# Group 0's outputs in the Strassen scheme of the other groups, x sums inside it, mixes on the vector engine, last keys ahead of the scan

## The chip, the core and the metric

The kernel runs on one core of a Trainium2 chip. The core has five engines, each with an instruction queue of its own that it works off in order: PE (matrix products; the profile lists weight loads apart as PEld), DVE (vector), ACT (scalar), POOL (GpSimd) and SP, which here only issues transfers. They wait for each other through semaphores. SBUF is the on-chip memory with 128 partitions, PSUM the banks that PE writes to. The metric is the device time of one execution in microseconds, as a median over runs.

## What is computed

An attention block with a gated recurrence, and then a feed-forward block with three input weights:

```
f = sigmoid(f_logit)                       # batch 4, heads 8, time 768, head size 48
state = f[t][:, None] * state + outer(k[t], v[t])
y[t]  = q[t] @ state
x   = y as (3072 tokens, 384)
h   = max(x @ w1, x @ w2, x @ w3)          # w1, w2, w3: 384 x 768
out = h @ w_out                            # w_out: 768 x 384
```

The weights arrive as 64-bit floats; each is turned into 32 bits on the chip ("rounding").

## The kernel before

**Units.** The recurrence is worked off in 24 units `u` of 64 time steps by two batches (128 tokens). For a unit, `scan` turns the gates on DVE and forms their running products, `after` makes `kh` (keys times decay) and `before` makes `qh` (queries times decay); from unit 6 on both products are on POOL (L340, L351), and the keys, queries and gates are turned by DVE transposes (L296). `pairs` multiplies `kh` and `qh` on PE (L392) and masks the result on DVE into `at` (L395). `values` multiplies `at` by v (L411), `sums` brings the state up to date from the turned keys `ks` (L436), `finish` adds the old state's part (L500) and copies the result to `xT`. `ks` is made by `keys_by_blocks(u, n)` for n = 0 to 3, four DVE transposes of 32 rows each (L382).

**Groups.** Four units are a group of 512 tokens. The feed-forward block of a group is a Python generator that yields the cost of each piece of PE work; `fill(ns)` in the unit loop (L1023 to L1075) pulls pieces until its budget is used up, so PE's order is units' products with feed-forward pieces between. A unit has five fills: of EARLY = 2360 while group 0 is worked off (units 4 to 7), of PART after. All is in one hand-written order; nothing is moved by a scheduler.

**The first matrix is subtracted.** The maximum is taken relative to x @ w1: w2 and w3 are replaced by w2 - w1 and w3 - w1 (`apart`), h is the maximum of their products and 0, and x @ w1 @ w_out is added by one linear matrix w1 @ w_out, which `linear` computes on PE from turned pieces of w1 (`turn`). It is kept as `w_nat`, and as `w_lin` with its rows placed in the order of heads by `place`, a set of ten small copies that SP issues. `place` also puts w2 and w3 (`w_in[1]`, `w_in[2]`) into `placed[0]` and `placed[1]`, while `linear` runs.

**Group 0** (`ffn_first`): plain products for w2 and w3, rounding of the last weight pieces (`round_to`), `turn`, `linear`, then `outputs`: per 128 tokens nine products with 384 columns, six with w_out and three with `w_nat`, a copy on ACT and a store. Between these outputs POOL makes `mix_in` (four sums of placed input weights, L805) and `mix` (five differences of output weights, L587), for use from group 1 on.

**Groups 1 to 5** (`ffn`): `inputs_by_pairs` (L836) and `outputs_by_pairs` (L609) use Strassen's scheme, seven products of half-size matrices in place of eight, over the halves of h's rows and the halves of w_out's columns. Its mixed weights are `w_mix`, kept in the space of `w_in[2]` and one tile of their own; its mixed h are `s_mix`, in the space of `w_in[1]`, made by `sums_of_hm` with four POOL operations per pair of h blocks (L596). The linear part, x by `w_lin`, is added by plain products, three per tile: 66 products of 192 columns per group. Sums that a product needs twice are copied from PSUM by ACT (`read`, L614) into `partial`, and added by DVE (`add`, L617) or POOL (L662). The products accumulate in the PSUM banks a, b, c; a is written on after it is read.

**What sets the order around the change.** SP issues all transfers in program order. DVE's order in a unit is: `ks` parts 0, 1 and 2, `at`, gate, scan, `ks` part 3, turned keys, second scan, turned queries, state.

Of the kernel before, what the change touches and what calls it, by code (L numbers as in the profile page):

```python
# [9 lines left out]
FP32 = mybir.dt.float32  # L10
# [3 lines left out]
ALU = mybir.AluOpType  # L14
# [32 lines left out]
C = 64  # L47
# [8 lines left out]
def kernel(  # L56
# [12 lines left out]
    nc = tc.nc  # L69
# [8 lines left out]
    GRP = 4  # L78
# [11 lines left out]
    def fast():  # L90
        ctx = ExitStack()
        with ctx:
# [137 lines left out]
            BY_VECTOR = 3  # L230
# [3 lines left out]
            def round_begin(n):  # L234
                if n in raw:
                    lo, hi = words(n)
                    top = tops[:, n % 4].bitcast(U32)
                    if n >= BY_VECTOR:

                        nc.scalar.activation(top.bitcast(FP32), hi.bitcast(FP32), AF.Sign)  # L240
                        nc.scalar.mul(top.bitcast(FP32), top.bitcast(FP32), -2.0)

                    rest = rests[:, n % 3].bitcast(U32)
                    nc.scalar.activation(rest, lo, AF.Copy, scale=2.0 ** -29)
                    halfway[n] = (top, rest)

            def round_end(n):
                if n in raw:
                    (top, rest), (_, hi) = halfway.pop(n), words(n)
                    if n < BY_VECTOR:  # L250
                        nc.vector.tensor_scalar(top, hi, 3, 0x3FFFFFF8, op0=ALU.logical_shift_left, op1=ALU.bitwise_and)
                        nc.vector.scalar_tensor_tensor(top, hi, 0xC0000000, top, op0=ALU.bitwise_and, op1=ALU.bitwise_or)
                    else:
                        nc.vector.scalar_tensor_tensor(top, hi, 3, top, op0=ALU.logical_shift_left, op1=ALU.bitwise_xor)  # L254

                    dst = pieces[n][0].bitcast(U32)
                    by = lambda t: t.rearrange("p (a c) -> p a c", a=dst.shape[1])
                    nc.gpsimd.tensor_tensor(dst, by(top), by(rest), op=ALU.add)  # L258
                    raw.pop(n)
# [297 lines left out]
            def outputs(hm, xT, i):  # L557
                p = bank()
                t = slice(i % 2 * UT, (i % 2 + 1) * UT)
                terms = [(hm[:, j, i * UT:(i + 1) * UT], w_out[:, j, :]) for j in range(NJ)]  # L560
                terms += [(by_halves(xT)[:, i // 2, k, t], w_nat[:, k, :]) for k in range(NK)]
                for n, (lhsT, rhs) in enumerate(terms):
                    nc.tensor.matmul(p[:, 0:DM], lhsT=lhsT, rhs=rhs, start=(n == 0), stop=(n == NJ + NK - 1))  # L563
                    if n % NK == NK - 1:
                        if n == NJ + NK - 1:
                            o = o_four[:, i]
                            nc.scalar.copy(o, p[:, 0:DM])
                            store(i, o)
                        yield NK * DM * COLUMN

            HJ, HD = NJ // 2, DM // 2
            corner = lambda k, n: w_out[:, k::2, n * HD:(n + 1) * HD]
            w_mix = [keep.tile([128, HJ, HD], FP32, name="mix")] + [w_in[2][:, :, n * HD:(n + 1) * HD] for n in range(4)]
            s_mix = [w_in[1][:, n, :].rearrange("q (jj t) -> q jj t", jj=HJ) for n in range(NK)]
            partial = [w_in[0][:, n, 0:DM] for n in range(NK)]
            pairs_of = lambda t: t.rearrange("q (p c) -> q p c", p=2)  # L580

            def mix(n):

                dst, x, y = ((w_mix[2], corner(1, 1), corner(0, 1)), (w_mix[0], corner(0, 1), corner(0, 0)),
                             (w_mix[1], corner(1, 1), w_mix[0]), (w_mix[3], corner(1, 0), w_mix[1]),
                             (w_mix[4], w_lin[:, :, 0:HD], w_lin[:, :, HD:]))[n]
                nc.gpsimd.tensor_tensor(dst, x, y, op=ALU.subtract)  # L587

            def sums_of_hm(hm, jj):

                first, second = ([hm[:, 2 * jj + k].rearrange("q (p n t) -> q n p t", p=2, n=2)[:, n] for n in range(2)]
                                 for k in range(2))
                s1, s2, s4 = (pairs_of(t[:, jj]) for t in s_mix)
                for dst, x, y, op in ((s1, first[1], second[1], ALU.add), (s2, s1, first[0], ALU.subtract),
                                      (first[1], first[0], first[1], ALU.subtract), (s4, second[0], s2, ALU.subtract)):
                    nc.gpsimd.tensor_tensor(dst, x, y, op=op)  # L596

            def outputs_by_pairs(g, hm, xT):
                tile_of = lambda p, n: slice((2 * p + n) * UT, (2 * p + n + 1) * UT)
                A = lambda k, n: lambda p: hm[:, k::2, tile_of(p, n)]  # L600
                X = lambda n: lambda p: xT[:, 0:NK, tile_of(p, n)]
                s1, s2, s4 = (lambda p, t=t: t[:, :, p * UT:(p + 1) * UT] for t in s_mix)
                lin = [w_lin[:, :, n * HD:(n + 1) * HD] for n in range(2)]
# [3 lines left out]
                def into(b, p, lhs, rhs):  # L607
                    for k in range(HJ):
                        nc.tensor.matmul(b[:, p * HD:(p + 1) * HD], lhsT=lhs(p)[:, k], rhs=rhs[:, k],  # L609
                                         start=id(b) not in begun, stop=(k == HJ - 1), skip_group_check=True)  # L610
                        begun.add(id(b))
# [7 lines left out]
                COST = HJ * HD * COLUMN  # L619
                a, b, c = bank(), bank(True), bank(True)  # L620
                into(b, 0, X(0), lin[0])
                yield COST
                into(b, 1, X(0), lin[0])
                yield COST
                into(a, 0, A(0, 0), corner(0, 0))
                yield COST
                into(b, 0, A(1, 0), corner(1, 0))
                yield COST
                into(a, 1, A(0, 0), corner(0, 0))
                read(a, 0)  # L630
                yield COST
                into(b, 1, A(1, 0), corner(1, 0))
# [3 lines left out]
                yield COST  # L636
                into(a, 0, s2, w_mix[1])
                yield COST
                into(a, 1, s2, w_mix[1])
                read(a, 1)  # L640
                yield COST
                d = b if last else c
                into(c, 0, s1, w_mix[0])
# [4 lines left out]
                into(d, 1, s1, w_mix[0])  # L648
# [5 lines left out]
                into(a, 0, A(0, 1), w_mix[2])  # L654
                yield COST
                into(a, 1, A(0, 1), w_mix[2])
                yield COST
                into(a, 0, X(1), lin[1])
                yield COST
# [3 lines left out]
                if last:  # L663
                    store_part(g, 1, 1)
                yield COST
                into(c, 0, X(0), lin[1])
                yield COST
                into(d, 1, X(0), lin[1])
                yield COST
                into(a, 0, A(1, 1), w_mix[3])  # L670
                yield COST
                into(a, 1, A(1, 1), w_mix[3])
# [3 lines left out]
                into(a, 0, X(1), w_mix[4])  # L676
                yield COST
                into(a, 1, X(1), w_mix[4])
# [3 lines left out]
                yield COST  # L682
                into(c, 0, s4, corner(1, 1))
# [3 lines left out]
                into(d, 1, s4, corner(1, 1))  # L687
# [67 lines left out]
            def ffn_first(xT):  # L755
# [18 lines left out]
                for a in range(NK):  # L774
                    if a < 2:
                        for n in range(2 * NK + 2):
                            place(placed[a].bitcast(FP32), w_in[a + 1], n)
                    for cost in linear(a):
                        round_to(rounded[0] + 1)
                        yield cost  # L780
                for n in range(2 * NK + 2):
                    place(w_lin, w_nat, n)
                made = iter([lambda n=n: mix_in(n) for n in range(4)] + [lambda n=n: mix(n) for n in range(5)])
                for i in range(GRP):
                    for n, cost in enumerate(outputs(hm, xT, i)):
                        if i or n:
                            next(made, lambda: None)()
                        if i == GRP - 1 and n == 1 and 1 in packed:
                            sums_of_x(1)
                        yield cost  # L790
# [33 lines left out]
            def inputs_by_pairs(g, hm, xT):  # L824
# [57 lines left out]
                def fourth(n):  # L882
                    into(A[n], n, w_two[1][:, 1], t4)
                    yield COST
                    into(A[n], n, w_two[1][:, 2], t5)
                    nc.vector.scalar_tensor_tensor(out(n, 0), out(n, 0), 0.0, two(A[n]), op0=ALU.max, op1=ALU.max)
                    nc.vector.scalar_tensor_tensor(out(n, 1), out(n, 1), 0.0, u3, op0=ALU.max, op1=ALU.max)  # L887
                    sums_of_hm(hm, n)
                    yield COST
# [48 lines left out]
            EARLY = 2360  # L938
            PART = (33 * TOK + 22 * HJ * HD) * COLUMN / (5 * GRP)
# [4 lines left out]
            with tc.manual_schedule():  # L944
# [78 lines left out]
                for u in range(GRP, NU):  # L1023
# [22 lines left out]
                    if u + 2 < NU:  # L1046
                        load_v(u + 2)
                    if n < NU:
                        if n < BY_ROWS:
                            sigmoids(n)  # L1050
                        scan(n)
                    check_range(u - CHECKS, 0)
                    fill(part)
                    keys_by_blocks(u, 3)
# [293 lines left out]
```

## Time and profile before

| | us |
|---|---|
| median of three runs | 422.57 (422.08 to 423.26) |
| the profiled execution | 423.19 |
| its span, first to last instruction | 421.5 |
| PE busy | 401.8 |
| DVE busy | 275.0 |
| POOL busy | 241.9 |
| ACT busy | 178.8 |
| mean granted clock of PE | 0.994 of full speed |

Stages, from the windows of the profile: up to 86 us the first units and group 0's input products run, with PE busy 71.3 us; from 86 to 98.7 `linear`; to 127 group 0's outputs; then five groups of some 60 us each, of which the outputs take about 25; the last matmul ends at 416.5.

A line of the chain of waits names a start, a length, the engine and source line, and how many instructions were put together. A 32-bit matmul is two records in it. A line of a timeline has the start, the length, the engine, line and operation, output and inputs with their shapes, and in brackets the idle time of the engine ahead of it with what ended that.

### The profile page before, as it was taken

To read this page: it belongs to the slowest core of one execution; us is meant where nothing else is said; L and a number is where in the kernel's file an instruction comes from. 1 tells how busy PE (TensorE), PEld (TensorE's weight loads), DVE (VectorE), ACT (ScalarE), POOL (GpSimd) and SP (SyncE) were. 2 spreads that over 40 slices of the span, in tenths; PEclk is the share of its full clock that TensorE was granted. 3 is DMA by queue.
4 is the path that set the end of the run, shared out by engine and by line. 5 is a ranking of instruction groups with operands and counts; after the bars stand their busy time and mean duration, and the time that the engine had idled before them with its cause. 6 is when DMAs were issued, how large, how long until landed. Compare 5 with 4: busy or idle time off the path is not lost.

```text
span 421.5 us, 11552 instructions
## 1 busy us (share of the span) xinstructions
PE 401.8 (95%) x4618; PEld 336.0 (80%) x4618; DVE 275.0 (65%) x549; ACT 178.8 (42%) x412; POOL 241.9 (57%) x266
## 2 busy tenths in 40 slices
PE   5978898899999999999999999999999999999995
PEld 4766764366668888998889988889988889988994
DVE  6995585897697699868789867889764730002300
ACT  2478576532114442425531444442254524577210
POOL 2189454744998676376586358576556960435600
PEclk9999999899999999999999999999999999999999
DMA  8999886677456763277645276725373010552012
GB/s 169 233 268 268 241 225 92 84 152 153 82 114 90 120 144 54 71 92 110 118 111 110 42 116 80 155 65 94 55 147 94 13 54 10 154 143 75 1 21 60
DMA packets 181562, 47.21 MB, mean 112 GB/s; under 512 B 160448, under 2 KB 179200, under 8 KB 181504
## 3 DMA queue, kind: packets, MB, share of 16 engines
q1 hardware_dynamic: 178032, 45.62, 52.9%
q10 hardware_dynamic: 3472, 0.81, 0.9%
q8 instruction: 37, 0.61, 0.6%
q14 instruction: 21, 0.17, 0.1%
HBM read 37.75 MB, written 4.72 MB: 101 GB/s over the span
## 4 chain that ended last, share of the span: by engine, by line
PE 87%; SPq 3%; DMA 3%; DVE 3%; ACT 1%; issue 1%; POOL 1%; DVEq 0%; ACTq 0%; POOLq 0%
PE p L836 19%; PE tr L836 16%; PE p L609 15%; PE tr L609 12%; PE p L537 6%; PE p L563 6%; PE y L411 3%; PE p L745 3%; PE y L500 3%; PE a L392 2%; PE y L436 2%; SPq L174 2%; DMA raw<-in_moe_w_dram 2%; DMA placed<-in_moe_w_dram 1%; SPq L164 1%
## 5 line engine op out<-in xcount | busy, mean ns | idle before, releaser
L382 DVE STREAM_TRANSPOSE ks<-kh 32x128 f32<-32x128 f32 x256 | 77.4, 302 | 5.1 <-POOL kh L340 1.0
L836 PE MATMUL tr<-xT,placed 128*128 128x256 f32 x300 | 73.4, 385 | 0.0
L836 PEld LDWEIGHTS tr<-xT,placed 128*128 128x128 f32 x300 | 55.6, 190 | 9.1 <-ACT hm L844 1.4
L836 PE MATMUL p<-xT,placed 128*128 128x256 f32 x180 | 45.0, 381 | 0.0
L537 PE MATMUL p<-xT,w_in 128*128 128x256 f32 (+1 forms) x108 | 36.2, 477 | 6.2 <-DVE hm L767 3.5
L340 POOL TENSOR_TENSOR kh<-kt,r 128x512 f32<-128x512 f32 x18 | 31.2, 1732 | 11.4 <-DVE kt L296 11.4
L617 DVE TENSOR_TENSOR o<-tr,w_in 128x384 f32<-128x384 f32 (+1 forms) x11 | 5.7, 514 | 48.8 <-PE tr L609 43.5
L836 PEld LDWEIGHTS p<-xT,placed 128*128 128x128 f32 x180 | 33.8, 190 | 4.7
L329 DVE TENSOR_TENSOR_SCAN r<-gate,from_one 128x520 f32<-128x520 f32 x24 | 31.5, 1312 | 8.2 <-ACT gate L308 5.1
L596 POOL TENSOR_TENSOR w_in<-hm 128x256 f32<-128x256 f32 x15 | 10.9, 724 | 40.2 <-DVE hm L887 40.2
L854 POOL TENSOR_TENSOR hm<-hm,rest_bits 128x512 f32<-128x512 f32 x15 | 23.0, 1533 | 18.8 <-ACT hm L844 18.8
L506 ACT COPY xT<-y 64x256 f32<-64x256 f32 (+1 forms) x60 | 22.1, 368 | 27.2 <-PE y L500 26.6
L537 PEld LDWEIGHTS p<-xT,w_in 128*128 128x128 f32 x108 | 19.9, 195 | 15.4 <-issue 8.6
L347 DVE TENSOR_TENSOR_SCAN prod<-gate,from_inv 128x520 f32<-128x520 f32 x24 | 32.2, 1340 | 0.0
L836 PE MATMUL p<-w_in,placed 128*128 128x256 f32 x120 | 30.0, 379 | 0.0
L258 POOL TENSOR_TENSOR w_in<-top_bits,rest_bits 128x384 uint32<-128x384 uint32 x18 | 22.1, 1233 | 13.1 <-DVE top_bits L254 8.1
L879 DVE TENSOR_TENSOR hm<-tr,hm 128x512 f32<-128x512 f32 x15 | 10.2, 681 | 29.0 <-PE tr L836 19.0
L662 POOL TENSOR_TENSOR o<-top_bits,w_in 128x384 f32<-128x384 f32 x5 | 5.1, 1014 | 41.6 <-ACT w_in L614 41.6
L395 DVE TENSOR_TENSOR at<-a,mask 128x512 f32<-128x512 f32 x24 | 16.5, 688 | 17.8 <-PE a L392 17.4
L614 ACT COPY w_in<-p 128x384 f32<-128x384 f32 x15 | 7.2, 478 | 47.3 <-PE p L609 47.3
L280 ACT ACTIVATE raw<-top_bits 128x384 f32<-128x384 f32 x48 | 25.2, 526 | 0.4
L836 PEld LDWEIGHTS p<-w_in,placed 128*128 128x128 f32 x120 | 22.8, 190 | 3.1
(155 smaller groups left out, 884.5 us busy)
## 6 DMA issues: line engine op xcount, KB each, us to landing
raw<-in_moe_w_dram SPq DMA_DIRECT2D x24, 384.0 KB, 3.9
v_ld<-in_v_dram SPq DMA_DIRECT2D x48, 96.0 KB, 3.2
placed<-in_moe_w_dram SPq DMA_DIRECT2D x12, 384.0 KB, 6.5
out_dram<-o SPq DMA_DIRECT2D x46, 96.0 KB, 2.2
placed<-in_moe_w_out_dram SPq DMA_DIRECT2D x6, 384.0 KB, 5.7
f_ld<-in_f_logit_dram SPq DMA_DIRECT2D x36, 64.0 KB, 2.6
k_ld<-in_k_dram SPq DMA_DIRECT2D x36, 64.0 KB, 2.6
q_ld<-in_q_dram SPq DMA_DIRECT2D x36, 64.0 KB, 2.5
```

The source lines that it names most:

```text
L258: nc.gpsimd.tensor_tensor(dst, by(top), by(rest), op=ALU.add)
L280: nc.scalar.activation(over, size, AF.Relu, scale=(-1 / HI_MIN, 1.0)[step - 1], bias=(1.0, -HI_END * (1 - 2.0 ** -24))[step - 1], accum_ou ...
L329: nc.vector.tensor_tensor_scan(r[:, 0:LEN][:, ::-1], flat(gate)[:, ::-1], flat(from_one)[:, ::-1], 1.0, op0=ALU.mult, op1=ALU.max)
L340: (nc.vector if u < BY_ROWS else nc.gpsimd).tensor_tensor(kh.rearrange("p h a t -> p a h t"), kt, by_batch(r[:, 1:LEN + 1].rearrange("p (x ...
L347: nc.vector.tensor_tensor_scan(flat(prod), flat(gate_tiles[u % 2]), flat(from_inv[u % 2]), 1.0, op0=ALU.mult, op1=ALU.max)
L382: nc.vector.transpose(ks[n * 32:(n + 1) * 32, :, par, e0:e0 + 32], kh[p0:p0 + 32, :, a, t0:t0 + 32])
L506: nc.scalar.copy(xT[o, :, t0 + a * C:t0 + (a + 1) * C], y[i, a, 0:HP * C].rearrange("p (h t) -> p h t", h=HP))
L537: nc.tensor.matmul(p if w < TOK else p.rearrange("p (two t) -> p two t", two=2), lhsT=w_in[i][:, kt, j * 128:(j + 1) * 128], rhs=x[:, t.st ...
L563: nc.tensor.matmul(p[:, 0:DM], lhsT=lhsT, rhs=rhs, start=(n == 0), stop=(n == NJ + NK - 1))
L609: nc.tensor.matmul(b[:, p * HD:(p + 1) * HD], lhsT=lhs(p)[:, k], rhs=rhs[:, k], start=id(b) not in begun, stop=(k == HJ - 1), skip_group_c ...
L836: nc.tensor.matmul(b[:, j * HALF:(j + 1) * HALF], lhsT=w[:, (2 * n + j) * 128:(2 * n + j + 1) * 128], rhs=x, start=begin and j == 0, stop= ...
L854: nc.gpsimd.tensor_tensor(out(n, 0), out(n, 0), first, op=ALU.add)
```

## The change

Group 0's outputs use `outputs_by_pairs` as well, with `mixed` false: h in the scheme and the linear part plain, by `w_nat`. Its `sums_of_hm` on POOL are put between the steps of `linear`, and the five `mix` operations go to DVE, in one block after `linear`; `w_mix[0]` now lies in w_out itself. In groups 1 to 5 two of the three x blocks enter the scheme as a fourth block, with weights `x_mix` (five DVE operations, `mix_x`, once in group 1) and sums of x (`sums_of_x_pair`, four DVE operations per group); only the third block stays plain, which makes 64 products. Inside the scheme the products of the last h block come later, and the s1 products ahead of the s2 products. The six w_out pieces are rounded with two DVE operations in place of two ACT and one DVE, two pieces per step of `linear`. `ks` part 3 goes ahead of the scan. EARLY and PART are made smaller.

```
-            BY_VECTOR = 3
+            BY_VECTOR = (*range(3), *range(3 * NJ, 4 * NJ))
...
-            w_mix = [keep.tile([128, HJ, HD], FP32, name="mix")] + [w_in[2][:, :, n * HD:(n + 1) * HD] for n in range(4)]
+            w_mix = [corner(0, 1)] + [w_in[2][:, :, n * HD:(n + 1) * HD] for n in range(4)]
+            x_mix = [w_lin[:, 0, HD:]] + [w_mix[4][:, n] for n in range(2)] + [keep.tile([128, HD], FP32, name="mix")]
...
+            s_last = keep.tile([128, HALF], FP32, name="s_last")
             def mix(n):
                 dst, x, y = ((w_mix[2], corner(1, 1), corner(0, 1)), (w_mix[0], corner(0, 1), corner(0, 0)),
                              (w_mix[1], corner(1, 1), w_mix[0]), (w_mix[3], corner(1, 0), w_mix[1]),
-                             (w_mix[4], w_lin[:, :, 0:HD], w_lin[:, :, HD:]))[n]
-                nc.gpsimd.tensor_tensor(dst, x, y, op=ALU.subtract)
+                             (w_mix[4], w_nat[:, :, 0:HD], w_nat[:, :, HD:]))[n]
+                nc.vector.tensor_tensor(dst, x, y, op=ALU.subtract)
+            def mix_x(n):
...
+                nc.vector.tensor_tensor(dst, x, y, op=ALU.subtract)
...
+            def sums_of_x_pair(xT, n):
+                sums_of_pair(xT[:, 0], xT[:, 1], *s_of_x(xT), part=slice(2 * n, 2 * n + 2), engine=nc.vector)
...
             def outputs_by_pairs(g, hm, xT):
...
+                mixed = g > 0
+                order = [*range(HJ - 1), *[HJ] * mixed, HJ - 1]
...
+                if mixed:
+                    sums_of_x_pair(xT, 0)
                 into(b, 0, X(0), lin[0])
...
+                early, rest = slice(len(order) - 1), slice(len(order) - 1, None)
+                for p in range(2):
+                    into(a, p, A(0, 0), C(0, 0), early)
+                    if mixed and p:
+                        sums_of_x_pair(xT, 1)
+                    yield COST - PART_COST
+                    into(b, p, A(1, 0), C(1, 0), early)
+                    yield COST - PART_COST
...
-                into(a, 0, s2, w_mix[1])
-                yield COST
-                into(a, 1, s2, w_mix[1])
-                read(a, 1)
-                yield COST
                 d = b if last else c
-                into(c, 0, s1, w_mix[0])
+                into(c, 0, s1, T(0))
...
+                into(a, 0, s2, T(1))
                 yield COST
-                into(a, 1, A(0, 1), w_mix[2])
+                into(a, 1, s2, T(1))
+                read(a, 1)
+                yield COST
+                into(a, 0, A(0, 1), T(2))
+                yield COST
+                into(a, 1, A(0, 1), T(2))
...
             def ffn_first(xT):
...
-                    for cost in linear(a):
-                        round_to(rounded[0] + 1)
+                    for n, cost in enumerate(linear(a)):
+                        round_to(rounded[0] + 2)
+                        if a and n < 2:
+                            jj = 2 * (a - 1) + n
+                            if jj < HJ:
+                                sums_of_hm(hm, jj)
                         yield cost
                 for n in range(2 * NK + 2):
                     place(w_lin, w_nat, n)
-                made = iter([lambda n=n: mix_in(n) for n in range(4)] + [lambda n=n: mix(n) for n in range(5)])
-                for i in range(GRP):
-                    for n, cost in enumerate(outputs(hm, xT, i)):
-                        if i or n:
-                            next(made, lambda: None)()
-                        if i == GRP - 1 and n == 1 and 1 in packed:
-                            sums_of_x(1)
-                        yield cost
+                for n in range(5):
+                    mix(n)
+                for n, cost in enumerate(outputs_by_pairs(0, hm, xT)):
+                    if 3 <= n < 7:
+                        mix_in(n - 3)
+                    yield cost
...
-            EARLY = 2360
-            PART = (33 * TOK + 22 * HJ * HD) * COLUMN / (5 * GRP)
+            EARLY = 2270
+            PART = (33 * TOK + 64 * HD) * COLUMN / (5 * GRP)
...
+                    keys_by_blocks(u, 3)
                     if n < NU:
...
                     fill(part)
-                    keys_by_blocks(u, 3)
```

## The prediction

> **What bounds the kernel now.** I read the page's busy shares first, then a table of windows by stage, then the chain of waits in order of time, then the timelines of the queues in the stage where the change adds waits.
>
> ```profile
> PE 401.8 (95%) x4618; PEld 336.0 (80%) x4618; DVE 275.0 (65%) x549; ACT 178.8 (42%) x412; POOL 241.9 (57%) x266
> ```
>
> ```profile
> 60.00:86.00 26.00, 22.51 (x242) 11.62 (x241) 19.52 (x33) 17.18 (x36) 15.79 (x15) 0.93 0.68 87
> 86.00:98.70 12.70, 12.70 (x161) 7.78 (x160) 12.25 (x29) 2.21 (x6) 6.22 (x6) 1.00 0.77 161
> 98.70:127.00 28.30, 28.30 (x330) 17.39 (x329) 21.38 (x49) 5.18 (x12) 22.74 (x16) 1.00 0.54 109
> 161.90:187.40 25.50, 25.50 (x326) 24.37 (x325) 19.64 (x42) 6.70 (x18) 15.19 (x18) 1.00 0.48 78
> ```
>
> These are windows of the whole core; the columns are the stretch, its length, then busy us of PE, PEld, DVE, ACT, POOL, the granted clock, the DMA share and GB/s. From 86 us on PE never idles: every column of matmul taken out is worth its time, and every new wait of PE costs its whole length. But DVE has 0.45 us left in 86 to 98.7, and there the change gives it more to do. The chain shows what the stage of the first group's outputs consists of:
>
> ```profile
> 98.74 1.94 PE p L563 x6
> 100.67 0.59 PE y L500 x32
> 101.27 0.47 PE a L392 x32
> 101.73 6.00 PE p L563 x18
> 107.74 0.62 PE y L411 x32
> 108.36 0.45 PE y L436 x32
> ...
> 127.03 0.86 PE p L836 x4
> ```
>
> A matmul stands here as two records, so nine 384-column matmuls take 6.00 us (0.667 each), and by the row `tr L609 x12` (1.95 us) a 192-column one takes 0.325. L411 and L436 at 107.74 are unit 7's values and state sums; they need DVE's masked product `at` of unit 7 and its turned keys. The timelines of SP's, DVE's and POOL's queues beside that:
>
> ```profile
> 96.69 5.65 SPq L461 DMA_DIRECT2D placed<-w_in  x8
> ```
>
> ```profile
> 95.29 3.77 DVE L382 STREAM_TRANSPOSE ks<-kh 32x128 f32<-32x128 f32 x12
> 101.81 0.69 DVE L395 TENSOR_TENSOR at<-a,mask 128x512 f32<-128x512 f32 x1 [2.74 <-PE a L392]
> ```
>
> ```profile
> 103.48 2.52 POOL L805 TENSOR_TENSOR placed<-placed 128x768 f32<-128x768 f32 x1 [6.29 <-DMA placed<-w_in]
> ```
>
> SP issues without a gap from 12.8 to 110 us, so the copies that read the third weight matrix (`place(placed[1], w_in[2])`) end when SP gets to them: the last is issued at 101.8 and lands 2.2 us later, at 104.0. POOL idled 6.29 us for the earlier ones, and nobody else minded.
>
> **The change, part by part.**
>
> Matmuls. Group 0's outputs go from 36 x 384 columns (24.0 us) to 66 x 192 (21.45): -2.55. Each later group goes from 66 to 64 of 192 columns: 5 x 0.65 = -3.25. In three groups the chain has 1.23 us where six matmuls need 0.97 (a first product waiting for DVE's last `hm`); the new order puts that product behind 3.9 us of others: 3 x 0.26 = -0.78.
>
> The mixes move from POOL to DVE, and this is the part that decides. `mix(0)` overwrites `w_in[2]`, so it may not start before the last `place(placed[1])` copy has read it: 104.0. In the changed kernel's compiled order the five mixes stand on DVE's queue behind unit 7's first eight key transposes (which end at 97.8 by the row above) and ahead of its third four, its `at` and its last four; DVE is in order, so all of these wait. PE meanwhile ends `linear` at 98.74 as before and has three matmuls (0.98), finish and pairs (1.06), eleven matmuls (3.58) and about 0.2 us of entry left: it needs `at` at 104.6, or earlier if less is lost before 98.74.
>
> Length of the five mixes: a DVE product of 384 elements from two SBUF inputs takes 0.55 us (L715, median 552 ns), one of 512 takes 0.68 (the same kind, L887), so 576 take about 0.75: 3.75 together. But POOL is then in the twelve new `sums_of_hm` operations (0.73 each, L596), and the two engines exclude each other:
>
> ```profile
> 54.00 1.19 POOL L258 TENSOR_TENSOR w_in<-top_bits,rest_bits 128x384 uint32<-128x384 uint32 x1 [1.24 <-DVE top_bits L254]
> ```
>
> ```profile
> 54.25 1.36 DVE L254 SCALAR_TENSOR_TENSOR top_bits<-raw,top_bits 128x384 uint32<-128x384 uint32 x1
> ```
>
> The 0.55 us operation ended 0.42 after POOL's end. POOL starts the sums after unit 7's `qh` (96.4) and the first copies: eight take it to 102.3, a state product 0.83, four more to 106.1. So at 104.0 it has 0.6 us of one and two more to go, which alternate with the mixes: 0.6 + 4 x 0.62 + 0.65 + 2 x 0.73 = 5.2, ending at 109.2. Bounds: 3.75 (no overlap) and 3.75 + 12 x 0.73 (all twelve in between), far apart; I take 5.2, which is near the first, because most of the sums run while DVE waits.
>
> Then four transposes 1.25 (109.2 to 110.45), `at` 0.69 (111.15), four transposes 1.25 (112.4), the sums of unit 7 ending at 112.9. PE is idle for 6.6 us and then half a unit. This is what such an idle time did at 73 to 79, in PE's timeline and in a window of PE alone (length, PE busy, clock, DMA share, GB/s):
>
> ```profile
> 74.98 4.51 PE L537 MATMUL p<-xT,w_in 128*128 128x512 f32 x6 [2.22 <-DVE hm L767]
> ```
>
> ```profile
> 76.00:77.00 1.00, 1.00 (x3) 0.50 0.62 91
> ```
>
> After 2.22 us of idle time the granted clock was 0.50 for 3.5 us, and three matmuls of 0.86 took 4.51: 1.93 lost. I take 1.8 for the same here; bounds 0 and 1.93.
>
> The Trainium skill (TensorE: Matmul & The Clock Gate, "What's actually happening") puts the drop at an idle window of about 3.4 us and the recovery at as much sustained work. By it the 2.22 us above should have been free and were not; the row decides. For the idle time worked out here it would give an estimated 1.7 us of loss, and so a sum lower by 0.1.
>
> A second new wait: ACT's copy `read(a, 1)` now stands directly ahead of the products that accumulate into the same bank (before, the s1 products stood between). The chain has this form at 83.68: 0.02 to the copy, 0.49, 0.14 back = 0.65 us. In the compiled order groups 1 to 4 have finish and pairs (1.06 us) between, which cover it; group 0 and the last have nothing: 2 x 0.65, bounds 0 and 0.7 each. After `read(a, 2)` two products (0.65) remain as cover: 0, at most 0.1 a group.
>
> From 112.9 PE still has 50 matmuls of group 0 (16.25), finish and pairs (1.06), values and sums (1.07), entries (0.6), the copy (0.65) and the slow clock (1.8): it begins group 1 at 134.3, where it began at 127.03. That is +7.3, with group 0's saving inside.
>
> Costed at nothing: the w_out rounding loses 12 ACT operations and gains six DVE ones of 0.50 (L251), in a stretch after which PE waits at `at` of unit 7 anyway; likewise whatever the smaller EARLY and the earlier values do to the stall of 2.22. Four x sums per group on DVE (4 x 0.41 by L767's 256 elements = 1.65) and five `mix_x` in group 1 (5 x 0.35, L617's 192 elements): DVE had 19.64 of 25.5 us busy there, and `at` was ready 4 us before its use (162 against 166.07), the s1 products come 5.8 us after the sums begin; if that cover is gone each group pays up to 1.6. The last keys ahead of the scan delay scan and `kh` by at most 1.25 us, with some 3 us between `qh` (108.76 to 109.94) and its pairs (115.41). On POOL the mixes go (8.0 us) and the sums come (8.9). Unit 8's `qh` follows DVE's keys at 112.4 by gate 0.70, scan 1.24, reciprocal 0.2, `kt` 0.7, second scan 1.2, the rest of `kh` 0.98 and its own 1.18: 118.6, with pairs of unit 8 at 120. `mix_in` (7.9, L805) follows until 126.5, with first readers past 136; then 1.2 for the scan that shares POOL's time, state 0.8, L662 1.0, ends 0.2, `kh` 1.7 and `qh` 1.2 bring unit 9's `qh` at 132.6; its pairs come at 136.6. The eight stores of group 0 leave SP's queue at 117 to 125 and come back in group 1, where nothing waits for them. The tail of 5 us after the last matmul stays.
>
> **Sum.** +7.3 - 3.25 - 0.78 + 0.65 (last group's copy) = +3.9. The profiled execution took 423.19 us around a span of 421.5, so it would become 427.1; the median of the runs, 422.57, lies 0.6 lower and becomes 426.5.
>
> **Rivals.**
>
> A, the gain in full (10%). If the mixes are ready before PE needs `at`, only the matmul terms are left: -2.55 - 3.25 - 0.78 + 1.3 = -5.3, 417.3 us. For it speaks that PE is the bound with no idle time from 86 on. It decides from the point where `mix(0)` starts by 104.6 - 0.69 - 1.25 - 3.75 = 98.9, five us before the last read of `w_in[2]` lands; SP's gapless queue speaks against that.
>
> B, the wait is there but cheap (14%). No overlap with POOL (-1.4), full clock (-1.8), both copies covered (-1.3): -0.6, 422.0 us; one of the three alone leaves it slower. Against it stand the three rows above. It holds from -0.6 to +1.3.
>
> C, it spreads (8%). POOL and DVE fall so far behind that unit 8's or 9's `qh` comes late too: `qh` of unit 8 has 1.4 us to spare and that of unit 9 4.0. Add the last copy landing after 4.6 us (the longest of L461) instead of 2.2, +2.4, and 1.7 for a late `qh`: +8, 430.6 us and above.
>
> **How the numbers follow.** The forecast has 68%: the order on DVE's queue and the landing of the copies are sure, the length of the mixes and the clock less so. 0.3% (1.3 us) is about what a measurement of this kernel can tell. Faster: A and 4 of B's 14, 0.14. Same: 10 of B's, 0.10. Slower: 0.76. The range leaves out A and C: from just below B's end, 421.5, to 430.6; the forecast's own is 423.9 to 430.6.
>
> **What would show it.** DVE idle from about 98 to 104 ahead of the first mix, released by the `placed` copies; the five mixes over 5 us or so with POOL's sums between; PE idle 6 to 7 us ahead of unit 7's values, released by `at`, and a clock near 0.5 after it; the first L836 product near 134. In groups 1 to 5 the outputs 0.65 us shorter with PE still full; 0.65 us of idle time on ACT's copy in the last group. Wrong if DVE reaches `at` of unit 7 before 106, or if PE shows new idle time in groups 1 to 4.

## The result, and the profile after

The changed kernel takes 431.72 us (median, 431.16 to 433.0) against 422.57: 1.022 times as long, with a 95% interval of 1.0205 to 1.0236. The forecast was 426.5, slower, with 421.5 to 430.6 as its range: the sign was right, the size less than half, and the result lies 1.1 us above the range. The profiled execution took 431.16 us around a span of 429.4, so the span grew by 7.9 us where +3.9 was worked out. (The medians lie 9.2 apart: the execution profiled after the change is the fastest of its three, the one before lies 0.6 above its median. What follows accounts for the 7.9.) Busy times of the changed kernel, from its page:

```profile
PE 402.3 (94%) x4658; PEld 343.7 (80%) x4658; DVE 300.9 (70%) x587; ACT 173.3 (40%) x401; POOL 245.3 (57%) x274
```

PE has as much busy time as before, although matmuls worth 5.8 us were taken out: part of it is time at half clock. DVE has 26 us more. The stages of the changed kernel in windows of the whole core (length, then busy us of PE, PEld, DVE, ACT, POOL, granted clock, DMA share, GB/s):

```profile
60.00:86.00 26.00, 22.92 (x307) 12.19 (x307) 22.04 (x38) 12.50 (x27) 15.58 (x16) 1.00 0.69 89
86.00:100.10 14.10, 12.57 (x94) 7.30 (x95) 11.66 (x25) 1.49 (x3) 8.48 (x10) 0.88 0.83 170
100.10:134.50 34.40, 29.74 (x389) 27.90 (x388) 26.12 (x50) 6.13 (x14) 26.71 (x26) 0.90 0.45 77
169.40:196.20 26.80, 25.78 (x321) 23.96 (x321) 24.73 (x53) 6.78 (x19) 13.83 (x15) 1.00 0.45 74
```

From 86 us on PE was full before, at clock 1.00. Now it lacks 1.5 us in `linear`, 4.7 in group 0's outputs and 1.0 in group 1's, and the clock is 0.88 and 0.90 in the first two. PE's own timeline shows the stops:

```profile
84.64 0.91 PE L766 MATMUL p<-w_out,w_in 128*128 128x384 f32 x2 [0.75 <-POOL w_out L258]
86.89 0.91 PE L766 MATMUL p<-w_out,w_in 128*128 128x384 f32 x2 [1.33 <-POOL w_out L258]
88.44 5.19 PE L766 MATMUL p<-w_out,w_in 128*128 128x384 f32 x10 [0.64 <-POOL w_out L258]
...
110.80 1.13 PE L411 MATMUL y<-at,v_ld 64*64 64x64 f32 x32 [4.09 <-issue]
...
120.00 1.24 PE L621 MATMUL p<-w_in,hm 128*128 128x192 f32 x6 [0.57 <-ACT rest_bits L626]
...
176.48 1.19 PE L621 MATMUL p<-w_out,hm 128*128 128x192 f32 x4 [1.02 <-DVE hm L909]
...
367.43 0.92 PE L621 MATMUL p<-w_in,hm 128*128 128x192 f32 x4 [0.54 <-ACT w_in L626]
...
414.15 0.92 PE L621 MATMUL p<-w_in,hm 128*128 128x192 f32 x4 [0.57 <-ACT w_in L626]
```

The reason for the longest and for the one at 176 stands in DVE's timeline:

```profile
95.55 2.50 DVE L382 STREAM_TRANSPOSE ks<-kh 32x128 f32<-32x128 f32 x8
103.23 1.21 DVE L570 TENSOR_TENSOR w_in<-w_out 128x576 f32<-128x576 f32 x1 [5.17 <-DMA w_in<-w_in]
...
108.72 1.25 DVE L382 STREAM_TRANSPOSE ks<-kh 32x128 f32<-32x128 f32 x4
110.01 0.69 DVE L395 TENSOR_TENSOR at<-a,mask 128x512 f32<-128x512 f32 x1
...
152.24 1.97 DVE L578 TENSOR_TENSOR w_in<-w_in 128x192 f32<-128x192 f32 x3
...
166.53 0.98 DVE L578 TENSOR_TENSOR mix<-w_in,w_in 128x192 f32<-128x192 f32 x1
167.43 0.88 DVE L578 TENSOR_TENSOR w_in<-w_in 128x192 f32<-128x192 f32 x1
...
171.57 0.69 DVE L395 TENSOR_TENSOR at<-a,mask 128x512 f32<-128x512 f32 x1
...
175.75 0.68 DVE L909 SCALAR_TENSOR_TENSOR hm<-hm,p 128x512 f32<-128x512 f32 x1
```

The mix block lies where the prediction had it: DVE stands 5.2 us for the copies, the five mixes take from 103.23 to 108.7, and `at` of unit 7 ends at 110.7. (The bracket names `w_in<-w_in`, the copies that follow next on SP's queue. By the trace's times from issue to landing, the last `placed<-w_in` copy, issued at 100.1, landed 3.0 us later, at 103.1, and the two `w_in<-w_in` copies issued next took 3.0 us or more from 100.7 on: it is the last reader of `w_in[2]` that set DVE free.) In group 1 there is no bracket at all from 151 to 182: DVE never idles, and gets to the last `hm` 1.0 us too late.

The start of each group's first input product, from PE's timeline (the chain of waits, which the prediction quotes, gives starts 0.16 later), says how the 7.9 us are spread:

| | before | after | change | forecast |
|---|---|---|---|---|
| begin of group 1 | 126.86 | 134.34 | +7.48 | +7.3 |
| group 1 | 60.41 | 61.65 | +1.24 | -0.91 |
| group 2 | 60.50 | 59.80 | -0.70 | -0.91 |
| group 3 | 60.50 | 59.79 | -0.71 | -0.91 |
| group 4 | 57.60 | 57.80 | +0.20 | -0.65 |
| group 5, to the last matmul | 50.60 | 50.98 | +0.38 | 0 |

The first row is the forecast's; the other five make 0.4 where -3.4 was worked out. So two things had to be tested: whether the first row has the cause that was given for it, and what took the gain of the groups.

### The profile page after: what moved, and what is told of

Same layout as the page of the kernel before. It is cut to its first block, busy times and chain, and to the rows that moved or that the text cites. A ratio compares the mean times of both kernels' runs of the same rounds, so it can differ in the third digit from the quotient of the medians.

```text
span 429.4 us, 11666 instructions
## 1 busy us (share of the span) xinstructions
PE 402.3 (94%) x4658; PEld 343.7 (80%) x4658; DVE 300.9 (70%) x587; ACT 173.3 (40%) x401; POOL 245.3 (57%) x274
## 4 chain that ended last, share of the span: by engine, by line
PE 76%; DVE 10%; SPq 4%; issue 3%; DMA 2%; POOL 2%; ACT 1%; ACTq 0%; DVEq 0%; POOLq 0%
PE p L859 16%; PE p L621 16%; PE tr L859 14%; PE tr L621 13%; PE p L537 4%; PE y L411 3%; PE p L766 2%; PE y L500 2%; DVE ks L382 2%; SPq L174 2%; PE a L392 2%; PE y L436 2%; DMA raw<-in_moe_w_dram 2%; DVE r L329 1%; SPq L164 1%
## 5 line engine op out<-in xcount | busy, mean ns | idle before, releaser
L339 POOL COPY ends<-r 128x8 f32<-128x8 f32 x24 | 8.2, 340 | 60.6 <-DVE r L329 60.6
L537 PE MATMUL p<-xT,w_in 128*128 128x256 f32 (+1 forms) x108 | 34.5, 460 | 4.6 <-POOL w_in L736 2.2
L340 POOL TENSOR_TENSOR kh<-kt,r 128x512 f32<-128x512 f32 x18 | 32.4, 1802 | 9.6 <-DVE kt L296 7.4
L586 POOL TENSOR_TENSOR w_in<-hm 128x256 f32<-128x256 f32 x18 | 13.4, 745 | 40.2 <-DVE hm L910 25.4
L621 PE MATMUL p<-w_in,hm 128*128 128x192 f32 x144 | 31.1, 338 | 1.7 <-ACT w_in L626 1.1
L347 DVE TENSOR_TENSOR_SCAN prod<-gate,from_inv 128x520 f32<-128x520 f32 x24 | 30.7, 1279 | 0.0
L621 PE MATMUL tr<-w_out,w_in 128*128 128x192 f32 x144 | 29.5, 333 | 0.0
L621 PE MATMUL p<-w_in,xT 128*128 128x192 f32 x124 | 27.0, 326 | 0.0
L621 PEld LDWEIGHTS p<-w_in,hm 128*128 128x128 f32 x144 | 23.5, 189 | 4.0 <-ACT w_in L626 2.5
```

The lines of the kernel that those rows point to most:

```text
L340: (nc.vector if u < BY_ROWS else nc.gpsimd).tensor_tensor(kh.rearrange("p h a t -> p a h t"), kt, by_batch(r[:, 1:LEN + 1].rearrange("p (x ...
L347: nc.vector.tensor_tensor_scan(flat(prod), flat(gate_tiles[u % 2]), flat(from_inv[u % 2]), 1.0, op0=ALU.mult, op1=ALU.max)
L537: nc.tensor.matmul(p if w < TOK else p.rearrange("p (two t) -> p two t", two=2), lhsT=w_in[i][:, kt, j * 128:(j + 1) * 128], rhs=x[:, t.st ...
L586: engine.tensor_tensor(dst, x, y, op=op)
L621: nc.tensor.matmul(b[:, p * HD:(p + 1) * HD], lhsT=x, rhs=w, start=id(b) not in begun, stop=True, skip_group_check=True)
```

## The experiments

Times are medians; each ratio is to executions of the kernel before that were made beside them on the same chip, with its 95% interval. The changed kernel itself was timed once, so "less" and "more" compare it with runs made later; the kernel before lay between 422.30 and 422.66 in all these sets.

**The mixes two places later.** Same block, same engine, same memory:

```
-                for n in range(5):
-                    mix(n)
...
                     keys_by_blocks(u, 3)
+                    if u == 2 * GRP - 1:
+                        for m in range(5):
+                            mix(m)
```

> The five mixes stay on DVE, stay in the third input weight's space and stay one block, but stand behind unit 7's masked product and last keys instead of in the middle of them. If the block's place on DVE's queue is what stops PE for 4.1 us at 106.7 and then halves the clock, the values of unit 7 start near 106.7, the clock stays at 1, and the first input product of group 1 comes at 134.5 - 4.1 - 1.8 = 128.6: about 5.9 us off, 425.8. If PE would be stopped there anyway (by the late rounding of w_out, or by POOL's sums of h), the first input product stays later than 132 and the time within 2.5 us of 431.7.

Measured: 425.83 us, ratio 1.0086 (1.0058 to 1.0114), 5.9 less than the changed kernel. In PE's timeline unit 7's values have no idle time ahead of them and full length, and group 1 begins at 128.31:

```profile
106.80 0.69 PE L411 MATMUL y<-at,v_ld 64*64 64x64 f32 x32
```

`linear` ran at half clock for as long as in the changed kernel (5.18 us for the ten records shown above with 5.19), so the comparison is clean: the place of the block is what costs the 5.9 us. One new stop came in, 0.41 us for unit 8's queries, which now stand behind the mixes.

**The mixes in memory that nobody is copying from.**

```
-            w_mix = [corner(0, 1)] + [w_in[2][:, :, n * HD:(n + 1) * HD] for n in range(4)]
+            w_mix = [corner(0, 1)] + [placed[2].bitcast(FP32)[:, :, n * HD:(n + 1) * HD] for n in range(4)]
...
-            w_sum = [placed[2].bitcast(FP32)[:, n] for n in range(NK)]
+            w_sum = [w_in[2][:, n] for n in range(NK)]
```

> The five mixes stay where the change puts them on DVE's queue, but write into the third placed tile, and the mixed input weights of POOL take the space of the third input weight instead: the mixes need no longer wait for the copies. If the wait for the copies is what makes the block costly, DVE works through it from 98.1 to about 103, the masked product is ready at 105.1 for 106.7, and the gain is that of the moved block, 5.9 us, 425.8. If the length of the mixes (5.5 us, shared with POOL) is enough by itself, the masked product comes at 107.5 or later, PE stops for 1 to 2 us, and the gain is 3 to 4 us.

Measured: 423.88 us, 1.0033 (1.0015 to 1.0052), 7.8 less: more than was expected of either. DVE now works from 97.79 on, `at` begins at 104.65, and PE's timeline shows two small stops, and, ahead of them, a `linear` at full clock:

```profile
88.15 3.49 PE L766 MATMUL p<-w_out,w_in 128*128 128x384 f32 x10 [0.64 <-POOL w_out L258]
...
105.44 0.69 PE L411 MATMUL y<-at,v_ld 64*64 64x64 f32 x32 [0.71 <-ACT rest_bits L626]
...
106.70 0.66 PE L436 MATMUL y<-v_ld,ks 64*64 64x48 f32 x26 [0.34 <-DVE ks L382]
```

These ten records took 5.19 in the changed kernel's profile, behind the same three stops. That is worth 1.7 of the 7.8 us, and belongs to the clock: the edit changes nothing ahead of that point. The length of the mixes alone still costs 1.05 us, because PE now arrives 2.0 us earlier.

**Only one mix waits.** The first mix stays in its place, the other four go behind unit 7's last keys:

```
-                for n in range(5):
-                    mix(n)
+                mix(0)
...
+                        for m in range(1, 5):
+                            mix(m)
```

> The changed kernel with only the first mix in its place among unit 7's keys, where it waits for the copies, and the other four behind unit 7's last keys. The wait stays whole (DVE stands from 98 to 103 or so), 4.3 us of its length go. If wait and length must come together to stop PE, the masked product is ready at 103.2 + 1.2 + 1.25 + 0.7 = 106.4, just ahead of 106.7, PE stops for less than 0.8 us at full clock, and the time is 425.8 to 426.6. If the wait alone is enough, PE stops for 2 us or more, and the time is 428 or more.

Measured: 426.64 us, 1.0113 (1.0087 to 1.0139). The wait was whole (first line, DVE), and PE stopped for 1.54 and 0.35 (second line, PE):

```profile
103.65 1.00 DVE L570 TENSOR_TENSOR w_in<-w_out 128x576 f32<-128x576 f32 x1 [5.40 <-DMA w_in<-w_in]
```

```profile
106.76 0.70 PE L411 MATMUL y<-at,v_ld 64*64 64x64 f32 x32 [1.54 <-ACT rest_bits L626]
```

`at` ended at 106.7, as worked out, but PE was there at 105.2, since `linear` had kept its clock here too. For the PE of the changed kernel, which came at 106.7, neither the wait (`at` at 106.7 here) nor the length (`at` at 105.3 with the mixes in their own memory) would alone have made `at` late; together they make it 4.1 us late. Two more stops of 0.71 and 0.41 us follow in this run, for unit 8's state and queries, which the four moved mixes delay.

**Matmuls in the gap.** Eight products whose result nobody uses, ahead of unit 7's values (`busy(8)` when `u == 7`).

> The changed kernel with eight more matmuls of 256 columns (0.43 us each, 3.5 together; their result is not used) on PE directly ahead of unit 7's values, where it otherwise idles for 4.1 us. If the half clock after that place comes from the idle time alone, the clock stays at 1, unit 7's values take 0.5 us in place of 1.1, and the first input product of group 1 comes at 134.5 - 1.8 = 132.7: 429.9. If the clock falls for another reason, or the work is simply lost time, it stays at 134.5 or comes later: 431.7 or more.

Measured: 429.66 us, 1.0177 (1.0142 to 1.0211), 2.1 less. Not all of that is the filler's: in its profile `linear` kept its clock too (3.49 us for the ten records), and the first mix began 0.8 us later than in the changed kernel, so that unit 7 went on at 111.54. The stretch that shows the filler is the one from the start of unit 7's values to group 1: 21.58 us, where the changed kernel has 23.54. PE's timeline, and the window behind it in PE alone (length, busy, clock, DMA share, GB/s), first in the changed kernel and then with the filler:

```profile
105.58 3.62 PE L957 MATMUL p<-from_one,ident 128*128 128x256 f32 x16
111.54 0.69 PE L411 MATMUL y<-at,v_ld 64*64 64x64 f32 x32 [2.35 <-issue]
```

```profile
110.00:115.00 5.00, 4.20 (x70) 0.50 0.66 89
110.00:115.00 5.00, 3.12 (x74) 1.00 0.63 90
```

The granted clock of a whole execution was 0.989 to 1.000 in the four runs with the filler, and 0.985 in all three of the changed kernel. Useless work in an idle stretch made what follows faster: the half clock was the price of the idle time, 2.0 us, as put down from the kernel before (1.8).

**The linear weight's mixes on POOL.** In `mix_x`, `nc.vector` becomes `nc.gpsimd`.

> The five mixes of the linear weight in group 1 are made by POOL in place of DVE, at the same points of the program. If they are what makes group 1 last 61.65 us where groups 2 and 3 last 59.80 (DVE without a gap from 151 to 182, and PE stopped for 1.02 us at 175.5 for hm), group 1 falls to about 59.8: 1.8 us off, 429.9. If the x sums and the last keys ahead of the scan fill DVE there by themselves, as they do in groups 2 and 3 without a stop, at most 0.5 us goes.

Measured: 430.88 us, 1.0204 (1.0175 to 1.0233). The runs of the two kernels overlap, since the moment at which unit 7 goes on differs by a microsecond (109.69 here, 110.80 in the changed kernel's profile); the groups of the profile are sharper: group 1 takes 59.69 in place of 61.65, groups 2 to 5 are unchanged to 0.01. DVE reaches the last `hm` 38.3 us into the group, not 41.4, and the stop is gone. Five operations of 192 columns were what group 1 lost.

**The old order of s2 and s1.** (s1, s2 and s4 are the mixed forms of h that the scheme multiplies.) The five lines of the s2 products go back ahead of `d = b if last else c`.

> The s2 products go ahead of the s1 products again, as before the change, in all groups. If the copy of the sum behind s2 costs what the profile shows (0.57 us of idle time in group 0, 0.54 in group 4, 0.57 in the last, each with 0.1 of a slow first product), these 2.0 us go, and the copy of the first sum, which then has two products as its cover, costs 0.2 in each of six groups: about 0.8 us off, 430.9. If the copies were covered by something else next in line, nothing moves, 431.7.

Measured: 431.42 us, 1.0203 (1.0171 to 1.0234), 0.3 less. The stops of group 0 and of the last group went; groups 2, 3 and 4 became 0.17 to 0.19 longer, which is the first copy with two products as its cover. But group 4's stop stayed:

```profile
367.84 0.92 PE L621 MATMUL p<-w_in,hm 128*128 128x192 f32 x4 [0.58 <-ACT w_in L626]
```

The next record of the same timeline reads `mix`, the last mixed weight: this stop, in both kernels, is at the fourth product block, behind `read(a, 2)`, and not behind s2. The expectation had named the wrong copy. What makes it late is ACT's queue in group 4, which the changed kernel's timeline of ACT shows:

```profile
362.19 0.48 ACT L626 COPY w_in<-p 128x384 f32<-128x384 f32 x1 [1.61 <-PE p L621]
362.82 1.14 ACT L506 COPY xT<-y 128x256 f32<-128x256 f32 x3
363.99 0.69 ACTq L519 DMA_DIRECT2D xT<-xT  x1
364.72 0.56 ACT L278 ACTIVATE top_bits<-raw 128x384 f32<-128x384 f32 x1 [0.77 <-ACT xT L506]
...
366.92 0.46 ACT L626 COPY w_in<-p 128x384 f32<-128x384 f32 x1
```

The copy behind s2 is at 362.19 and in time. Then come the last unit's x, a DMA that ACT itself issues, and operations that check the range of the raw weights (L278, L280); the next copy is 0.5 us late.

**x plain in groups 1 to 5.** `mixed` is always false, with one difference of 576 columns in place of the five mixes and PART set for 66 products.

> The changed kernel with x plain in groups 1 to 5, as before the change: 66 output products per group, no x sums, and one operation of 0.75 in place of the five mixes of the linear weight. If the x blocks save 0.65 us a group on PE and their operations stop PE in group 1 alone, groups 2 and 3 become 0.65 longer each, 60.45, group 1 falls from 61.65 to about 60.5, and the time is 431.7 + 4 x 0.65 - 1.2 = 433.1. If the x sums on DVE stop PE a little in every group, those groups grow by less than 0.3 and the time falls below 431.

Measured: 434.66 us, 1.027 (1.024 to 1.0301), 2.9 more. Group 1 takes 60.91, groups 2 and 3 60.91 and 60.92: 0.7 less and 1.1 more than with the x blocks; all five groups together take 2.4 more. (The other part stands ahead of group 1, which the edit does not touch: it begins 1.5 us later, at 135.82, and the ten records of `linear` took 6.48 us in this profile.) Groups 2 and 3 grow by more than two matmuls, because the copy behind s2 is now uncovered in every group:

```profile
182.39 2.22 PE L625 MATMUL p<-w_in,hm 128*128 128x192 f32 x12 [0.57 <-ACT w_in L630]
```

With 64 products a unit's finish and pairs fall between that copy and its reader, with 66 they fall elsewhere. In this kernel the x blocks are worth 2.4 us, that cover included.

**All of it together.** Mixes in the third placed tile, two in place and three behind unit 8's scan, `mix_x` on POOL, and s4 products as cover for the copies:

```
                 into(a, 1, s2, T(1))
                 read(a, 1)
                 yield COST
+                into(c, 0, s4, C(1, 1))
+                yield COST
...
                 read(a, 2)
...
-                into(c, 0, X(0), lin[1])
...
+                else:
+                    into(d, 1, s4, C(1, 1))
```

(the x products of c and d go to the end; in the last group they stay, and the second s4 product is last).

> The changed kernel with the mixed weights in the third placed tile, two mixes where they stood and three behind unit 8's scan, the linear weight's mixes on POOL, and another order of the output products: behind the s2 products and the copy of their sum one s4 product of 1.3 us, behind the copy of the next sum the other. If the terms found so far are all there is, the span falls from 422.0 (own space) by 1.9 (group 1), 2.0 (three copies), 1.0 (0.2 in each of five groups) and 0.5 (waits of unit 7's values): 416.6, and the time to 418.5, 4 us below the kernel before. If ACT itself is late in group 4, its 0.5 stays: 419. If taking these waits away only uncovers others, 421 or more.

Measured: 418.57 us, 0.9899 (0.9876 to 0.9922), with a span of 416.9 where 416.6 was summed. Groups 2 and 3 take 59.60, group 4 56.95 (its stop is gone: 1.3 us cover it). The terms add up, with one new stop among them: 0.61 us for unit 8's queries.

**And w_out rounded with ACT.** `BY_VECTOR` is 0 to 2 alone again.

> The last kernel, with the w_out pieces rounded by two ACT operations and one DVE operation, as before the change. If DVE's second operation per piece is what holds up POOL's rounding from 84 to 88, where PE waits 2.7 us in three places, at least 1.5 us of that goes, and the time falls by 1 to 3 us below the run with all the edits together, to about 416.5. If it is the order of the pieces and POOL's own operations (1.0 us each), nothing is gained: within 0.7 us of that run.

Measured: 416.18 us, 0.9846 (0.982 to 0.9873): 2.4 less, and the fastest kernel of this study, 6.5 us below the kernel before beside it (422.66). Behind 60 us PE has three stops left, two of 0.61 and this one, in place of the three at 84 to 88:

```profile
81.98 1.53 PE L773 MATMUL p<-w_out,w_in 128*128 128x384 f32 x4 [1.66 <-POOL w_out L258]
```

**The two parts that the prediction had passed over.** In this fastest kernel, EARLY at 2360, and in another run the last keys behind scan and fill, as before the change:

> The last kernel of the call before (all edits, w_out pieces rounded with ACT) with EARLY at 2360 again, its value before the change. If the smaller EARLY is what took the 2.22 us stop at 72.8 and the half clock behind it out of the kernel before (it puts two more input products ahead of the product that waits for hm), both come back, up to 3.5 us, while PE's wait of 1.7 for the rounding at 82 goes: about 2 us slower, 418.2. If they went for another reason, it stays within 0.7 us of 416.2.

> The same kernel with the last keys of a unit behind its scan and first fill again, as before the change. If their place costs and brings nothing, as the prediction had it, the time stays within 0.7 us of 416.2. If with the fuller DVE the keys would come too late for the state sums, PE stops in several units and the time rises by 1 us or more; if instead the earlier scan lets POOL make the queries earlier and more is gained, it falls by 0.7 or more.

Measured: 424.33 us (1.0057, 1.0036 to 1.0078) and 424.48 us (1.0047, 1.0027 to 1.0066). Each costs 8 us, four times what was expected of the first; the prediction had counted nothing for the second. PE's timeline with EARLY 2360, then the same with the keys behind, and a window of PE alone behind that stop:

```profile
75.00 4.51 PE L537 MATMUL p<-xT,w_in 128*128 128x512 f32 x6 [2.22 <-DVE hm L795]
...
117.31 0.66 PE L500 MATMUL y<-qh,state 48*48 48x64 f32 x32 [2.55 <-DVE st L444]
...
192.16 1.13 PE L868 MATMUL p<-xT,w_in 128*128 128x256 f32 x4 [1.11 <-POOL xT L852]
```

```profile
165.23 0.31 PE L436 MATMUL y<-v_ld,ks 64*64 64x48 f32 x2 [1.37 <-DVE ks L382]
165.89 0.66 PE L436 MATMUL y<-v_ld,ks 64*64 64x48 f32 x26 [0.34 <-DVE ks L382]
```

```profile
166.40:170.00 3.60, 3.60 (x17) 0.53 0.49 136
```

EARLY brings back the stop of 2.22 with its half clock, and sets the later pieces of the feed-forward block differently against the units: a new stop for the state, and stops for POOL's sums of x in groups 2, 3 and 4. Group 1 begins 5.5 us later, and groups 2 to 4 take 2.4 more together. With the keys behind, DVE makes the first two x sums (1.28 us) ahead of them, and PE waits for the keys in its state sums, 1.7 us in group 1 with half clock after it, and 1.1 in each of groups 2 and 3; these three groups take 4.2, 1.9 and 1.9 more.

**The same two alone, in the kernel before.**

```
-            EARLY = 2360
+            EARLY = 2270
```

> The kernel before with one number changed: EARLY 2270 in place of 2360. If that number alone removes the 2.22 us stop at 72.8 and the half clock behind it, 4.1 us go there; PE then reaches the first linear product some 4 us earlier and waits up to 2 us for the rounding of w_out: 1.5 to 4 us faster in all, about 420. If the shift sets later pieces of the groups against the units (as EARLY at 2360 did to the kernel with all edits, in the other direction), new stops of 0.5 to 1 us come in each group and the time is 422 or more.

> The kernel before with the last keys of a unit ahead of the next unit's scan, as the change has it, and nothing else. If their place matters only where DVE carries the x sums as well, the time stays at 422.5, within 0.7. If it shortens PE's wait at 72.8 or for the state sums in the first units, it falls by 0.7 us or more; if the scan, 1.25 us later, makes POOL's queries late in the groups, it rises by 1 us or more.

Measured: 430.80 us (1.019, 1.0157 to 1.0223) and 427.47 us (1.0134, 1.0095 to 1.0174). Alone, both make the kernel before slower, by 8.2 and 4.9. First EARLY, then the keys, in PE's timeline:

```profile
89.65 6.30 PE L745 MATMUL p<-w_out,w_in 128*128 128x384 f32 x10 [3.32 <-POOL w_out L258]
...
170.81 0.59 PE L609 MATMUL p<-w_out,hm 128*128 128x192 f32 x2 [1.35 <-DVE hm L886]
```

```profile
74.61 2.81 PE L537 MATMUL p<-xT,w_in 128*128 128x512 f32 x6 [2.22 <-DVE hm L767]
...
165.08 0.59 PE L609 MATMUL p<-w_out,hm 128*128 128x192 f32 x2 [1.48 <-DVE hm L886]
```

With EARLY 2270 the 2.22 us stop is down to 0.61, and 1.67 and 3.32 for the rounding come in its place. In both, the last `hm` of groups 1 to 3 is 1.35 to 1.84 us late for the first product that reads it. The changed kernel has that product 3.9 us further back in its order; groups 2 and 3 show no such stop there. So these parts seem to belong together; what each of the two is worth inside the changed kernel itself was not run, and stays open.

## Why the prediction was half right

**The mix block: right.** "The part that decides" decided: the place on DVE's queue, the copies (103.2 for 104.0), the mixes in turn with POOL (5.5 for 5.2), the half clock (2.0 for 1.8) and the begin of group 1 (134.50 in the chain, for 134.3) came out, and moving the block or freeing its memory takes 5.9 us or more away. Alone, a mix took 0.75 to 0.76 us, as estimated. Inside the sum one value was off without effect: PE idled 4.1 us and not 6.6, mostly because it came 2.1 later. `linear` ended 1.3 later, and 16 matmuls stand ahead of unit 7's values where the prediction counted three and eleven (with its 50 behind, that makes 64 of the 66). Neither reached the total, because PE waited there anyway: the wait hid them.

**The w_out rounding "costed at nothing": right for this kernel only.** PE lost 2.7 us at 84 to 88, and 1.7 by the clock, and regained 1.6 of the 2.22 and its half clock. `linear` ended 1.3 later, and the wait for `at` covered it. Without the mix block rounding with ACT is worth 2.4.

**Failed: "four x sums per group on DVE and five `mix_x` in group 1" costed at nothing.** The mixes were priced at 1.75 from L617's 0.35, an operation with one input in PSUM; with both in SBUF and POOL at work they took 3.8. And the cover of 4 us was that of `at` alone. In group 1 it shrank to 0.6 (`at` ended at 172.26 and was read at 172.90), and the last `hm`, which stands behind `at` on DVE's queue, came 1.0 us late even for a reader that had been put back by 3.9 us. Group 1 lasted 2.15 longer than forecast; without the five mixes on DVE it lasts 59.69. The x sums themselves stopped nobody in groups 2 and 3.

**Failed: "after `read(a, 2)` two products remain as cover: 0, at most 0.1 a group".** The stop was 0.2 in groups 2 and 3: with s4 products as cover they fall from 59.80 to 59.60. In group 4 ACT's queue makes it 0.85, and the last group has 0.4 of it, half of that behind the copy priced at 0.65, which took 0.83 there. These 1.6 us and group 1's 2.15 are what the forecast missed, but for the 0.2 of the first row.

**Right: that the copy behind s2 stops PE in group 0 and in the last group, and is covered in groups 1 to 4.** Also right was what would show the forecast wrong: new idle time in groups 1 to 4, and there it is, in 1 and 4.

**The rivals.** A fell with the row at 103.23; B with the 5.5 us of the mixes, the clock of 0.50 behind them and the two copies' stops of 0.57. C names the time that came (430.6 and above), but not its way: neither unit 8's nor unit 9's queries stopped PE.

## What to carry to other kernels

An operation that is put on an engine's queue costs what everything behind it in the queue costs when it waits. Here either a later place or memory that nobody else was reading took most of that cost away. "Hidden" work on an engine that is full for 30 us is not hidden: add up the engine's whole stretch, for each result that somebody waits for, with durations from the rows where the other engine is at work, before a term is set to zero. In a hand-ordered kernel a budget or the place of four transposes was worth as much here as the change itself, with a sign that depended on the rest, so such parts are priced with everything else in, not alone.

## What was not expected of the hardware

The same idle time on PE is sometimes followed by half clock and sometimes not. Nine profiles have the stops of 0.75 and 1.33 in `linear`, eight of them also the third, of 0.64. The ten records behind that took 3.49 us in four (own memory, one waiting mix, filler, all together), 5.2 in three (the changed kernel, the mixes later, `mix_x` on POOL) and 6.48 with x plain; in the ninth, with the old order of s2 and s1, the half clock began behind the second stop already and cost 0.9. The 2.22 us stop at 72.8 was followed by 4.51 in the kernel before and by 2.81 with the keys moved; 1.7 us were enough at 165, and 2.35 behind the filler were not. The Trainium skill (TensorE: Matmul & The Clock Gate, "What's actually happening") says that the activity window runs freely, which would fit the irregularity, though no run here tests it; it asks for an idle window of about 3.4 us, and the drops here came after 1.7 and 2.2.

A DVE operation of 192 columns with two SBUF inputs took 0.66 to 0.98 us in group 1, with POOL at work on SBUF data beside it, where one of 576 took 0.75 to 0.76 with POOL idle.
